# Normalising every second attention head on ScalarE in the last four batches

## The chip, the core and the metric

The kernel runs on one core of one Trainium2 chip, as one launch. A core has five engines, each with a queue of its own that it works off in order: PE (TensorE, matrix products and transposes, with the weight loads PEld beside it), DVE (VectorE), ACT (ScalarE), POOL (GpSimd) and SP (which here only issues DMAs). They wait for each other by semaphores. PE writes to PSUM, eight banks of 128 partitions x 2 KB, and DVE and ACT empty them. The metric is the device time of one execution, in microseconds; less is better.

## What is computed

Attention of 8 batches and 8 heads over 576 queries, with 16 extra "beacon" keys ahead of the 576 keys, causal over the latter; then a mixing of low rank along the sequence, and a two-layer network with ReLU over the channels, with a residual.

```python
def _attn_ref(q, k, v, beacon_k, beacon_v):          # q, k, v: 8 x 8 x 576 x 64
    k_all = np.concatenate([beacon_k, k], axis=2)    # 592 keys
    v_all = np.concatenate([beacon_v, v], axis=2)
    scores = scale * np.matmul(q, k_all.transpose(0, 1, 3, 2))
    scores = np.where(causal, -1000000000.0, scores)
    a = np.exp(scores - scores.max(-1, keepdims=True))
    a /= a.sum(-1, keepdims=True) + 1e-09
    return np.matmul(a, v_all)

def _moe_ref(x, U, V, w_ch1, w_ch2):                 # x: 8 x 576 x 512
    h = x.transpose(0, 2, 1) @ U @ V
    u = x + h.transpose(0, 2, 1)
    return u + np.maximum(u @ w_ch1, 0.0) @ w_ch2
```

## The kernel before

Heads are worked on in pairs: slot `p` is pair `p % 4` of batch `p // 4`, 32 slots in all. For a pair PE makes the transposed scores (`sps`, keys down the partitions, queries along the columns; L371 and, from the third batch on, L410 in `visit`), in four groups of blocks that lie in a bank each. ACT takes the exponential of each group into an `expt` buffer in SBUF (L419; 496, 464, 496 and 208 columns for groups 0 to 3). There are four such buffers, two slots' worth; `visit` may take groups of two neighbouring slots in one call, and group 3 of both shares a bank. DVE then takes the minimum with a mask over the diagonal blocks (L349), which sets masked entries to zero.

`av_unit` multiplies with the values. For one head it fills one bank, `po`, with five query tiles of 65 columns: 64 of the weighted sum, and one with the sum of the weights, since the values have a column of ones. DVE takes the reciprocal of the five sums (L436, 128x5, into the persistent tile `rec`), and multiplies all five tiles by it in one instruction (L437, 128x5x64, fp32 in PSUM to fp16 in `xb`, the batch's token-major attention result). With that the bank is given back.

Banks are handed out by `pst` in the order in which `emptying` gave them back, as the program is written. So each product that opens a new bank waits for the instruction that emptied that bank some steps before, on whichever engine that ran.

When a batch's four pairs are done, `turn_x` has SP transpose `xb` by DMA into `uT` (L456); DVE adds the product of low rank to it (L477). The network then runs in blocks of 512 tokens, as a queue of small units. `fill(n)` takes n of them and writes them between the parts of a slot, so that PE has work while ACT and DVE prepare the next pair. In the batches concerned a block is made with seven half-size products in place of eight, in both layers. Names that the steps below use:

- `gps` (L675): a bank of the first layer, turned into `gT` by a Relu on ACT (L683) or DVE (L681);
- `qpsA`, `qpsD`, `qpsF` (L701): banks of the first layer's seven-product form. `qpsA` grows from product to product, and after each ACT copies its state out (L720, into `kept` or `st`), which must be done before PE adds the next product to it; DVE adds that copy to `qpsD` and `qpsF` (L723), ACT ends `qpsA` with a Relu (L756);
- `mpsA` to `mpsF` (L829, L909): banks of the second layer; `mpsA` is copied out by ACT (L866, L919, L926), the others by DVE (L849).

From slot 12 on, `long_slot` sets the order by hand, by the pair's place in its batch. In the first and the second place (c = 0, 1) the `av` parts stand among `fill` calls. In the third (c = 2) the two parts are followed by `go([(p+1, 2), (p+2, 0)])`, four exponentials of 496 columns; in the fourth (c = 3) by `turn_x` and `go` with groups 2, 1 and the shared group 3, eight exponentials. The scheduler is told to keep the written order (`tc.manual_schedule`), so the order of each queue is that of the code.

Of the kernel before, what the change touches and what calls it, by code (L numbers as in the profile page):

```python
# [13 lines left out]
AF = mybir.ActivationFunctionType  # L14
ALU = mybir.AluOpType
# [3 lines left out]
P = 128  # L19
# [11 lines left out]
def kernel(  # L31
# [13 lines left out]
    nc = tc.nc  # L45
    B, H, S, D = q.shape
# [9 lines left out]
    scale = float(1.0 / (D ** 0.5))  # L56
# [6 lines left out]
    NT = NC  # L63
# [43 lines left out]
    def pst(shape, dtype, name):  # L107

        b = emptied.pop(0)
        t = psum.tile(shape, dtype, tag=f"bank{b}", name=name)  # L110
        bank_of[id(t)] = (b, t)
        return t

    def emptying(t):
        emptied.append(bank_of.pop(id(t))[0])
# [308 lines left out]
    def av_unit(b, h, ex, vs, xb):  # L424
        po = pst([P, NT, E], F32, name="po")
        for j in range(NT):
            for c in range(j + 1):
                nc.tensor.matmul(  # L428
                    po[:, j, :],
                    ex[0 : nk[c], ds(blk[(c, j)], P)],  # L430
                    vs[0 : nk[c], ds(c * H * E + h * E, E)],
                    start=(c == 0),
                    stop=(c == j),
                )
        r = rec[:, b * H + h, :, :]
        nc.vector.reciprocal(out=r, in_=po[:, :, D : D + 1])  # L436
        nc.vector.tensor_tensor(  # L437
            out=xb[:, :, ds(h * D, D)], in0=po[:, :, 0:D], in1=r.broadcast_to([P, NT, D]), op=ALU.mult
        )
        emptying(po)  # L440

    def x_into(xb, ups, cc, js, a, first):
# [798 lines left out]
    def av_of(p):  # L1241
        b, c = divmod(p, NH2)
        if c == 0:
            assert not coming or b < DT0
            xbs[b] = xbp.tile([P, NT, DM], F16, name="xb", tag="xb")
        return [
            lambda i=i: av_unit(b, 2 * c + i, expts_of(p)[i], vss[b % 2], xbs[b]) for i in range(2)
        ]
# [8 lines left out]
    DT0 = 4  # L1257
# [100 lines left out]
    with tc.manual_schedule(engines={ENG.PE, ENG.Activation, ENG.DVE, ENG.SP, ENG.Pool}):  # L1358
# [194 lines left out]
        for p in range(NP1, NP):  # L1553
            b, c = divmod(p, NH2)
# [75 lines left out]
    with tc.If(n_bad != 0, label="general"):  # L1630
        with tc.For_i(0, B, 1) as bi:
            L = qk_tiles()
            qT = qkt.tile([P, NH2, S], F16, name="qT", tag="qT")
            xb = xbp.tile([P, NT, DM], F16, name="xb", tag="xb")
# [45 lines left out]
```

## Time and profile before

| | |
|---|---|
| median of 3 runs | 331.51 us (331.44 to 334.58) |
| the profiled execution's own time | 331.11 us |
| its span in the trace | 329.4 us |
| granted TensorE clock | 1.00 throughout |

The profile is of one execution. Rows of a group give line, engine, operation, out<-in with shapes, count, busy us, mean ns of one, and the idle time before them with what ended it. Rows of the timeline give start, duration (of the merged instructions, where a count x2 or more stands behind), engine, line and shapes, and in brackets an idle time before the row and what ended it. Time counts from the start of the span. PEld is PE's weight load: it runs ahead of the products, so its waits need not hold them up. The four batches from `DT0 = 4` on have their `av` parts between 127.1 us and 258.6 us.

### The profile page before, as it was taken

The page shows a single profiled execution, that of the slowest core. Times are in us where ns is not written, and L with a number is a line of the kernel's source. Part 1 is how long each engine was busy: PE and PEld are TensorE (multiplying, and loading weights), DVE is VectorE, ACT ScalarE, POOL GpSimd, SP SyncE. Part 2 cuts the span into 40 slices and gives each one's busy share as a digit, 9 for nine tenths or more (in the row PEclk, how much of TensorE's full clock was granted, in tenths as well). Part 3 has the DMA queues.
Part 4 walks back from the last instruction along what each step waited for, and adds up shares of the span by engine and source line. Part 5 has one row for each costly group of instructions (what it writes and reads, how often), then busy time and mean ns, then how long its engine had stood idle before and what let it go on. Part 6 is the DMA issues. An engine that isn't in the chain of part 4 may idle for free.

```text
span 329.4 us, 9288 instructions
## 1 busy us (share of the span) xinstructions
PE 323.4 (98%) x3661; PEld 228.6 (69%) x3661; DVE 263.6 (80%) x610; ACT 196.8 (60%) x432; POOL 167.2 (51%) x263
## 2 busy tenths in 40 slices
PE   8899999999999999999999999999999999999996
PEld 4564555555578655876588878865777888788785
DVE  6676988668998577787778777877878998797994
ACT  5966962689972577447954796368726622722720
POOL 8985834568147960589148932960085036030030
PEclk9999999999999999999999999999999999999999
DMA  8999999999999994999999999795114321505104
GB/s 166 141 163 143 182 192 201 194 192 151 110 128 160 186 173 83 118 160 144 147 141 134 190 123 164 96 207 91 20 34 140 67 61 65 98 0 161 35 1 131
DMA packets 150558, 41.95 MB, mean 127 GB/s; under 512 B 131312, under 2 KB 149936, under 8 KB 150512
## 3 DMA queue, kind: packets, MB, share of 16 engines
q0 software_dynamic: 87568, 18.18, 75.1%
q1 hardware_dynamic: 62144, 22.41, 35.9%
q10 hardware_dynamic: 800, 0.75, 0.7%
q8 instruction: 29, 0.48, 0.6%
q14 instruction: 17, 0.14, 0.2%
HBM read 37.45 MB, written 9.44 MB: 142 GB/s over the span
## 4 chain that ended last, share of the span: by engine, by line
PE 93%; ACT 4%; DVE 1%; DMA 1%; issue 0%
PE gps L675 22%; PE po L428 9%; PE mpsA L909 9%; PE qpsA L701 6%; PE mpsD L829 6%; PE sps L410 6%; PE cps L1053 4%; PE gps L1027 4%; PE mpsE L829 3%; PE mpsC L829 3%; PE mpsB L829 3%; PE qpsD L701 3%; ACT expt L377 2%; PE mpsF L829 2%; ACT w L377 2%; PE mpsD L909 2%
## 5 line engine op out<-in xcount | busy, mean ns | idle before, releaser
L577 POOL TENSOR_TENSOR ob<-ob,ut 128x128 f32<-128x128 f32 x104 | 50.0, 511 | 120.7 <-DVE ob L849 59.4
L419 ACT ACTIVATE expt<-sps 128x496 f16<-128x496 f32 (+2 forms) x192 | 82.0, 539 | 41.8 <-PE sps L410 41.8
L675 PE MATMUL gps<-uT,w 128*128 128x512 f16 (+1 forms) x368 | 78.1, 351 | 0.0
L829 PEld LDWEIGHTS <-gT 128*128 128x128 f16 x576 | 54.3, 98 | 8.7 <-issue 2.6
L675 PEld LDWEIGHTS <-w 128*128 128x128 f16 x368 | 33.3, 98 | 25.6 <-issue 1.3
L653 DVE TENSOR_TENSOR gT<-gT 128x1024 f16<-128x1024 f16 (+3 forms) x87 | 47.0, 561 | 0.9
L239 POOL DMA_DIRECT2D vs<-in_v_dram x50 | 40.0, 817 | 14.2 <-DMA w<-in_moe_w_ch_dram 12.2
L683 ACT ACTIVATE gT<-gps 128x512 f16<-128x512 f32 x63 | 37.4, 617 | 16.0 <-PE gps L675 11.9
L428 PEld LDWEIGHTS <-expt 128*128 128x128 f16 x900 | 33.9, 98 | 8.4 <-issue 1.5
L428 PE MATMUL po<-vs,expt 128*128 128x65 f16 x900 | 36.4, 194 | 0.6 <-DVE expt L349 0.4
L909 PEld LDWEIGHTS <-gT 128*128 128x128 f16 x336 | 31.2, 98 | 3.9
L437 DVE TENSOR_TENSOR xb<-po,rec 128x320 f16<-128x320 f32 x64 | 31.4, 491 | 2.2
L349 DVE TENSOR_TENSOR expt<-expt,bigmask 128x768 f16<-128x768 f16 x56 | 31.3, 599 | 0.4 <-ACT expt L419 0.2
L720 ACT ACTIVATE kept<-qpsA 128x512 f32<-128x512 f32 x18 | 10.9, 603 | 24.0 <-PE qpsA L701 13.2
L410 PE MATMUL sps<-qT,kT 64*128 64x80 f16 (+4 forms) x288 | 22.6, 281 | 0.0
L436 DVE RECIPROCAL rec<-po 128x5 f32<-128x5 f32 x64 | 11.9, 186 | 13.0 <-PE po L428 12.8
L377 ACT ACTIVATE expt<-sps 128x496 f16<-128x496 f32 (+2 forms) x48 | 20.6, 584 | 0.7 <-PE sps L371 0.7
L909 PE MATMUL mpsA<-w,gT 128*128 128x256 f16 x160 | 19.1, 273 | 0.0
L410 PEld LDWEIGHTS <-kT 64*128 64x128 f16 x288 | 10.2, 94 | 12.8 <-issue 8.2
L681 DVE TENSOR_SCALAR gT<-gps 128x512 f16<-128x512 f32 x17 | 11.7, 689 | 8.9 <-PE gps L675 8.6
L1136 POOL DMA_DIRECT2D st<-in_q_dram x20 | 16.9, 868 | 1.0 <-DVE rec L436 0.4
L1136 POOL DMA_DIRECT2D st<-in_k_dram x20 | 16.9, 861 | 1.0 <-DVE pr L292 1.0
(165 smaller groups left out, 541.6 us busy)
## 6 DMA issues: line engine op xcount, KB each, us to landing
out_dram<-ob SPq DMA_DIRECT2D x33, 256.0 KB, 3.1
vs<-in_v_dram POOLq DMA_DIRECT2D x18, 128.0 KB, 6.9
w<-in_moe_w_ch_dram POOLq DMA_DIRECT2D x4, 512.0 KB, 6.6
w<-in_moe_w_ch_dram POOLq DMA_DIRECT2D x2, 1024.0 KB, 12.9
st<-in_k_dram POOLq DMA_DIRECT2D x12, 128.0 KB, 6.7
st<-in_q_dram POOLq DMA_DIRECT2D x12, 128.0 KB, 8.8
st<-in_k_dram POOLq DMA_DIRECT2D x4, 288.0 KB, 12.0
st<-in_q_dram POOLq DMA_DIRECT2D x4, 288.0 KB, 12.5
```

The source lines that it names most:

```text
L239: nc.gpsimd.dma_start(out=dst[a : a + nq[j], j, :, :], in_=src[hs, ds(q0[j], nq[j]), :].rearrange("h p d -> p h d"))
L377: nc.scalar.activation(out=ex[i][:, ds(AT[g], gw[g])], in_=ps[g, i][:, 0 : gw[g]], func=AF.Exp, scale=scale)
L410: nc.tensor.matmul(banks[i][:, ds(at0 + o, w)], kT(hp, c, ch), qT[hp, c, ds(qa, w)], start=True, stop=True, skip_group_check=len(unit) > 1,)
L419: nc.scalar.activation(out=at[p][3][i][:, ds(AT[g], gw[g])], in_=bank[:, ds(at0, gw[g])], func=AF.Exp, scale=scale)
L428: nc.tensor.matmul(po[:, j, :], ex[0 : nk[c], ds(blk[(c, j)], P)], vs[0 : nk[c], ds(c * H * E + h * E, E)], start=(c == 0), stop=(c == j),)
L577: nc.gpsimd.tensor_tensor(out=o[:, i, ds(c, w)], in0=x[:, i, ds(c, w)], in1=y[:, i, ds(c, w)], op=op)
L653: nc.vector.tensor_tensor(out=o[:, ds(d0, n)], in0=x[:, ds(d0, n)], in1=y[:, ds(d0, n)], op=op)
L675: nc.tensor.matmul(g[:, ds(o, w)], w1[:, cc, ts(dc, P)], uT[:, cc, ds(at, w)], start=(cc == 0 and o == 0), stop=(cc == NCC - 1), skip_grou ...
L683: nc.scalar.activation(out=cell["g"][:, dc, :], in_=g, func=AF.Relu)
L829: nc.tensor.matmul(ps, a()[:, d, ds(P * i, P)], bm[:, d, ds(c0, w)], start=fresh and d == 0 and i == 0, stop=d == HF - 1, skip_group_check ...
L909: nc.tensor.matmul(ps, a()[:, d, ds(P * i, P)], bm[:, d, ds(c0, w)], start=fresh and d == 0, stop=d == HF - 1, skip_group_check=True,)
L1136: coming.append(lambda d=dst, s=src, a=m[j] - nq[j], n=m[j], j=j: nc.gpsimd.dma_start(out=d[a:n, j, :, :], in_=s[:, ds(q0[j], nq[j]), :].r ...
```

## The change

From batch `DT0 = 4` on, the second head of each pair (`h % 2`) is multiplied by ACT. DVE still takes the reciprocal. In place of DVE's one instruction over all five query tiles there are five ACT copies of 128x64, one a tile, each with the tile's column of `rec` as a per-partition scale. The first head of each pair, the earlier batches and the fallback path stay as they are. These are 4 batches x 4 pairs = 16 heads: 16 DVE instructions go, 80 ACT instructions come.

```diff
         r = rec[:, b * H + h, :, :]
         nc.vector.reciprocal(out=r, in_=po[:, :, D : D + 1])
-        nc.vector.tensor_tensor(
-            out=xb[:, :, ds(h * D, D)], in0=po[:, :, 0:D], in1=r.broadcast_to([P, NT, D]), op=ALU.mult
-        )
+        if b >= DT0 and h % 2:
+            for j in range(NT):
+                nc.scalar.activation(
+                    out=xb[:, j, ds(h * D, D)], in_=po[:, j, 0:D], func=AF.Copy, scale=r[:, j, :]
+                )
+        else:
+            nc.vector.tensor_tensor(
+                out=xb[:, :, ds(h * D, D)], in0=po[:, :, 0:D], in1=r.broadcast_to([P, NT, D]), op=ALU.mult
+            )
         emptying(po)
```

Lines behind it have numbers higher by six in the changed file: L683, L720 and L756 are L689, L726 and L762 there.

ACT's queue at the end of slot 19 (the fourth pair of batch 4), before: the Relu that ends `qpsA`, then the eight exponentials of the next slots (numbers in the names are those of the buffers and banks), then three Relus.

```order
L756 ACTIVATE gT<-qpsA 128x2x256
L419 ACTIVATE expt_105<-sps_3128 128x496
L419 ACTIVATE expt_106<-sps_3129 128x496
L419 ACTIVATE expt_105<-sps_3136 128x464
L419 ACTIVATE expt_106<-sps_3137 128x464
L419 ACTIVATE expt_105<-sps_3140 128x208
L419 ACTIVATE expt_107<-sps_3140 128x208
L419 ACTIVATE expt_106<-sps_3141 128x208
L419 ACTIVATE expt_108<-sps_3141 128x208
L683 ACTIVATE gT<-gps 128x512 x3
```

The same place in the changed kernel:

```order
L762 ACTIVATE gT<-qpsA 128x2x256
L439 ACTIVATE xb<-po,rec 128x64 x5
L419 ACTIVATE expt_105<-sps_3144 128x496
L419 ACTIVATE expt_106<-sps_3145 128x496
L419 ACTIVATE expt_105<-sps_3152 128x464
L419 ACTIVATE expt_106<-sps_3153 128x464
L419 ACTIVATE expt_105<-sps_3156 128x208
L419 ACTIVATE expt_107<-sps_3156 128x208
L419 ACTIVATE expt_106<-sps_3157 128x208
L419 ACTIVATE expt_108<-sps_3157 128x208
L689 ACTIVATE gT<-gps 128x512 x3
```

The five copies stand ahead of the eight exponentials; nothing else has moved.

ACT's queue one slot earlier, at the end of slot 18 (the third pair), before:

```order
L720 ACTIVATE kept<-qpsA 128x512
L419 ACTIVATE expt_107<-sps_3015 128x496
L419 ACTIVATE expt_108<-sps_3016 128x496
L419 ACTIVATE expt_105<-sps_3023 128x496
L419 ACTIVATE expt_106<-sps_3024 128x496
L720 ACTIVATE kept<-qpsA 128x512
L683 ACTIVATE gT<-gps 128x512 x2
```

And in the changed kernel:

```order
L726 ACTIVATE kept<-qpsA 128x512
L439 ACTIVATE xb<-po,rec 128x64 x5
L419 ACTIVATE expt_107<-sps_3027 128x496
L419 ACTIVATE expt_108<-sps_3028 128x496
L419 ACTIVATE expt_105<-sps_3035 128x496
L419 ACTIVATE expt_106<-sps_3036 128x496
L726 ACTIVATE kept<-qpsA 128x512
L689 ACTIVATE gT<-gps 128x512 x2
```

Here they stand ahead of four exponentials and of the next copy of `qpsA`.

ACT's queue in the last two slots, 30 and 31, before:

```order
L720 ACTIVATE kept<-qpsA 128x512 x2
L683 ACTIVATE gT<-gps 128x512
L419 ACTIVATE expt_107<-sps_4912 128x496
L419 ACTIVATE expt_108<-sps_4913 128x496
L720 ACTIVATE kept<-qpsA 128x512
L683 ACTIVATE gT<-gps 128x512
L720 ACTIVATE st_115<-qpsA 128x512
L756 ACTIVATE gT<-qpsA 128x2x256
L720 ACTIVATE st_115<-qpsA 128x512
L683 ACTIVATE gT<-gps 128x512
L720 ACTIVATE st_115<-qpsA 128x512
```

And in the changed kernel:

```order
L726 ACTIVATE kept<-qpsA 128x512 x2
L439 ACTIVATE xb<-po,rec 128x64 x5
L689 ACTIVATE gT<-gps 128x512
L419 ACTIVATE expt_107<-sps_4972 128x496
L419 ACTIVATE expt_108<-sps_4973 128x496
L726 ACTIVATE kept<-qpsA 128x512
L689 ACTIVATE gT<-gps 128x512
L726 ACTIVATE st_115<-qpsA 128x512
L762 ACTIVATE gT<-qpsA 128x2x256
L726 ACTIVATE st_115<-qpsA 128x512
L689 ACTIVATE gT<-gps 128x512
L439 ACTIVATE xb<-po,rec 128x64 x5
```

The copies of slot 30 stand ahead of a Relu of `gps`, those of slot 31 ahead of the next copy of `qpsA` (the row that followed, `st_115<-qpsA`, comes behind them). DVE's queue loses one row at each of the sixteen places, PE's and SP's keep their order; where they waited for DVE's multiplication, for the bank or for `xb`, they wait for ACT.

## The prediction

> **What bounds the kernel now.** I read the page's busy times first, then the windows over the four batches that change, then who waits for whom there, then the timeline slot by slot. A slot is one head pair: 16 to 19 are batch 4, 20 to 23 batch 5, 24 to 27 batch 6, 28 to 31 batch 7. In the first row a number is busy time and a percentage its share of the span; in the second, PE's busy time stands first, DVE's third, ACT's fourth, and 1.00 is the granted clock; the third gives us in total, times, and the longest.
>
> ```profile
> PE 323.4 (98%) x3661; PEld 228.6 (69%) x3661; DVE 263.6 (80%) x610; ACT 196.8 (60%) x432; POOL 167.2 (51%) x263
> ...
> 125.00:263.00 138.00, 138.00 (x1609) 103.61 (x1609) 111.45 (x238) 86.40 (x189) 69.67 (x111) 1.00 1.12 122
> ...
> PEld L675 <- DVE xb L437: 0.9, 3, 0.5
> ...
> L437 DVE TENSOR_TENSOR xb<-po,rec 128x320 f16<-128x320 f32 x32 | 15.7, 491 | 1.1
> ```
>
> PE is busy for all 138.00 us of the stretch in which all sixteen changed heads lie. DVE's share there is 81% (111.45), ACT's 63% (86.40). PE waits for the operation that is moved, L437, three times, for 0.9 us together, and that is on its weight loads, which run ahead of the products. So faster vector work can give back 0.9 us at most, while every wait newly put in PE's way is lost for good: PE has no pause in which to catch up.
>
> **What is removed.** Half of the 32 rows of L437 go: 16 x 0.491 = 7.9 us of DVE. PE's stream hides them now, and they give nothing back. The sixteen reciprocals stay, in place.
>
> **What is added.** 80 ACT copies of 128x64. No ACT row before takes a per-partition scale, so the price is bounded by the nearest rows.
>
> ```profile
> L1189 ACT ACTIVATE kT<-tpb 128x16 f16<-128x16 f16 x1 | 0.2, 177 | 0.0
> ...
> L756 ACT ACTIVATE gT<-qpsA 128x512 f16<-128x512 f32 x6 | 3.6, 597 | 1.2 <-PE qpsA L701 1.2
> ...
> 245.10 0.34 ACT L419 ACTIVATE expt<-sps 128x208 f16<-128x208 f32 x1 [6.74 <-PE sps L410]
> ...
> 149.11 2.01 ACT L419 ACTIVATE expt<-sps 128x496 f16<-128x496 f32 x4 [1.44 <-PE sps L410]
> ...
> 155.43 2.90 ACT L419 ACTIVATE expt<-sps 128x496 f16<-128x496 f32 x8 [0.62 <-PE sps L410]
> ```
>
> Alone, 16 columns take 177 ns and 512 take 597: 0.85 ns a column, hence 177 + 48 x 0.85 = 218 ns for 64. Back to back they overlap: the second group of exponentials has 768 columns more than the first (2752 against 1984) and four instructions more, in 0.89 us more. 768 x 0.85 is 0.65; the other 0.24 is 0.06 an instruction. A 64-wide copy with full overlap then costs 0.06 + 0.054 = 0.115 us. The five copies so hold ACT for 0.58 us (full overlap) to 1.09 us (none). I take no overlap between copies, since each brings an operand of its own, whose overlap no row shows, but overlap between the last copy and the plain instruction behind it: 4 x 0.218 + 0.115 = 0.99 us. Were each as long as the next larger lone row, 0.34, it would be 4 x 0.34 + 0.115 = 1.48.
>
> The Trainium skill, "ScalarE: Activation LUTs", section "What ACT_TABLE_LOAD costs", gives 186 ns plus 0.833 ns a column with immediate operands, about 93 ns more for a pointer operand and about 93 ns of overlap back to back. By that, as an estimate, five copies hold ACT for 5 x 0.239 = 1.2 us, and the sum below would be 0.21 us dearer at each of eight places, 342.2 us in all. The trace agrees on the plain part (612 ns by the page for 512 columns, 597 in the row); no run here shows the pointer.
>
> **Where they stand.** ACT runs in order. At its place in the queue it now waits for the DVE reciprocal, then copies, and everything behind is late: exponentials, the copies of `qpsA` into `kept`, Relus, which PE needs for its banks and operands. The first copy can start about where L437 started (0.03 us after the reciprocal's end). So the delay of the next ACT instruction is L437's start + 0.99 - its present start.
>
> Third slot of a batch (18, 22, 26): four exponentials follow. First and last of the three:
>
> ```profile
> 149.12 0.18 DVE L436 RECIPROCAL rec<-po 128x5 f32<-128x5 f32 x1
> 149.33 0.49 DVE L437 TENSOR_TENSOR xb<-po,rec 128x320 f16<-128x320 f32 x1
> ...
> 150.98 0.63 ACT L720 ACTIVATE kept<-qpsA 128x512 f32<-128x512 f32 x1
> ...
> 151.82 0.60 PE L701 MATMUL qpsA<-st,lw 128*128 128x256 f16 x4
> ...
> 217.82 2.01 ACT L419 ACTIVATE expt<-sps 128x496 f16<-128x496 f32 x4 [1.48 <-PE sps L410]
> ...
> 218.00 0.49 DVE L437 TENSOR_TENSOR xb<-po,rec 128x320 f16<-128x320 f32 x1
> ```
>
> The delay is 149.33 + 0.99 - 149.11 = 1.21 and 218.00 + 0.99 - 217.82 = 1.17, 1.19 in the mean. ACT is busy without a gap to L720, so the delay reaches it whole. L720 ends at 151.61, and PE's next `qpsA` product, which adds to the bank that L720 reads, starts at 151.82: 0.21 less 0.03 for the hand-over is 0.18 of cover. PE loses 1.01 us, three times: 3.0.
>
> Fourth slot (19, 23, 27): eight exponentials follow, and the reciprocal comes after they could start.
>
> ```profile
> 156.17 0.49 DVE L437 TENSOR_TENSOR xb<-po,rec 128x320 f16<-128x320 f32 x1
> 156.69 6.95 SPq L456 DMA_TRANSPOSE uT<-xb  x5
> 156.72 2.27 PEld L675 LDWEIGHTS <-w 128*128 128x128 f16 x12 [0.47 <-DVE xb L437]
> 158.15 1.17 ACT L683 ACTIVATE gT<-gps 128x512 f16<-128x512 f32 x2
> 159.83 0.38 PE L410 MATMUL sps<-qT,kT 64*128 64x336 f16 x6
> ...
> 224.15 2.91 ACT L419 ACTIVATE expt<-sps 128x496 f16<-128x496 f32 x8 [0.62 <-PE sps L410]
> ...
> 224.66 0.49 DVE L437 TENSOR_TENSOR xb<-po,rec 128x320 f16<-128x320 f32 x1
> ...
> 226.87 1.17 ACT L683 ACTIVATE gT<-gps 128x512 f16<-128x512 f32 x2
> ...
> 228.40 0.38 PE L410 MATMUL sps<-qT,kT 64*128 64x336 f16 x6
> ```
>
> Delays: 156.17 + 0.99 - 155.43 = 1.73 and 224.66 + 0.99 - 224.15 = 1.50. The two Relus behind the exponentials end at 159.32 and 228.04 and free the banks that PE's score products take at 159.83 and 228.40; less the hand-over that is 0.48 and 0.33 of cover. PE loses 1.25 and 1.17, three times 1.21: 3.6. Within this lies the bank of `po` itself, which PE's weight load at 156.72 already awaits: it comes free at about 157.26, not 156.66. SP's transposes of `xb` start some 0.6 us later; DVE adds to what they write only some 15 us on (171.47 in the timeline):
>
> ```profile
> 171.47 1.82 DVE L477 TENSOR_TENSOR uT<-ups,uT 128x496 f16<-128x496 f32 x3
> ```
>
> Slots 30 and 31, the last two pairs, have other neighbours.
>
> ```profile
> 251.70 0.60 ACT L683 ACTIVATE gT<-gps 128x512 f16<-128x512 f32 x1 [0.73 <-PE gps L675]
> ...
> 252.40 0.49 DVE L437 TENSOR_TENSOR xb<-po,rec 128x320 f16<-128x320 f32 x1
> ...
> 253.12 0.62 ACT L720 ACTIVATE kept<-qpsA 128x512 f32<-128x512 f32 x1
> ...
> 253.77 0.69 DVE L723 TENSOR_TENSOR gT<-qpsD,kept 128x512 f16<-128x512 f32 x1 [0.88 <-ACT kept L720]
> ...
> 254.53 0.60 PE L701 MATMUL qpsD<-uT,lw 128*128 128x256 f16 x4
> ...
> 257.83 0.60 ACT L720 ACTIVATE st<-qpsA 128x512 f32<-128x512 f32 x1 [0.31 <-PE qpsA L701]
> ...
> 258.14 0.49 DVE L437 TENSOR_TENSOR xb<-po,rec 128x320 f16<-128x320 f32 x1
> ...
> 258.55 0.68 DVE L723 TENSOR_TENSOR gT<-qpsD,st 128x512 f16<-128x512 f32 x1
> ...
> 259.38 0.60 PE L701 MATMUL qpsD<-uT,st 128*128 128x256 f16 x4
> ```
>
> In 30 the delay is 252.40 + 0.99 - 251.70 = 1.69. It passes through L720 to DVE's L723, which waits for L720 now, and on to PE's `qpsD`: L723 ends at 254.46, PE starts at 254.53, 0.04 of cover. Loss 1.65. In 31 it is 258.14 + 0.99 - 257.83 = 1.30; L720 ends 0.12 before L723 starts, L723 0.15 before PE's `qpsD`, together 0.21 of cover. Loss 1.09.
>
> First and second slots (16, 20, 24, 28 and 17, 21, 25, 29) cost nothing:
>
> ```profile
> 164.73 0.49 DVE L437 TENSOR_TENSOR xb<-po,rec 128x320 f16<-128x320 f32 x1
> 165.14 0.38 ACT L919 ACTIVATE kept<-mpsA 128x256 f32<-128x256 f32 x1 [0.74 <-PE mpsA L909]
> ...
> 166.01 0.38 ACT L919 ACTIVATE kept<-mpsA 128x256 f32<-128x256 f32 x1 [0.49 <-PE mpsA L909]
> ...
> 174.01 0.49 DVE L437 TENSOR_TENSOR xb<-po,rec 128x320 f16<-128x320 f32 x1
> ...
> 176.53 0.81 ACT L419 ACTIVATE expt<-sps 128x208 f16<-128x208 f32 x3 [6.74 <-PE sps L410]
> ```
>
> In slot 20 the first L919 moves to 165.72, but the second waits for PE until 166.01 and absorbs it. In slot 21 ACT idles 6.74 us and the copies end at about 175.1, before 176.53. Were these covers gone, each block would cost up to 0.99.
>
> **Sum.** 3.0 + 3.6 + 1.65 + 1.09 = 9.4 us on the profiled execution's own 331.11: 340.5 us. That execution is 0.4 below the median of the runs, 331.51, so against that it is 2.7%.
>
> **Rivals.** (a) The copies hide: ACT's idle third takes them and PE's cover is enough. With all eight losses falling by 1 us per us of block, the total stays below 1% (3.3 us) only if the block is under 0.99 - (9.4 - 3.3)/8 = 0.23 us, 0.05 a copy, below the lower bound of 0.115. For it speaks only ACT's 63%; against it that ACT has no gap at the eight places. Time 331.5 to 334.8, not slower; chance 0.09. (b) Relief of DVE: it frees 7.9 us, but PE's waits for L437 cap the gain at 0.9: 330.2 us. More than 1% (3.3 us) would need PE waits that no row shows, against 138.00 of 138.00; I leave half of this rival's chance to it. Chance 0.04. The Trainium skill, "Perfetto Trace Analysis", section "Optimizing Scalar/DVE Operations", says that with DVE saturated some work may go to Scalar; its condition is not met at the eight places, where PE is the full engine. (c) Dearer copies, 1.48 a block: 0.49 more at eight places, 344.4 us; chance 0.13.
>
> **How the numbers follow.** The forecast has 0.74. With full overlap the block is 0.41 shorter, 3.3 us over eight places: 337.2; with none at all 0.10 longer: 341.3. The range 336.5 to 343.5 takes in both, a little more cover at the low end, and half of the way to (c). About 1% is what a measurement of this kernel can tell from no change. Faster has 0.02 (half of b), the same 0.11 (a and the rest of b), slower 0.87 (the forecast and c).
>
> **What would show it.** Right: PE idle or its loads waiting at 3 + 3 + 2 places, by about 1 us each, for ACT's copies, L720 or Relus; ACT 80 instructions more, of some 0.2 to 0.3 us; eight blocks of 0.6 to 1.1 us; nothing lost in first and second slots. Wrong: PE still without waits, blocks under 0.25 us, or PE waiting at places not named here, such as the transposes of `xb` or the masks behind the late exponentials.

## The result and the profile after

| | before | changed |
|---|---|---|
| median | 331.48 us | 341.56 us |
| lowest to highest | 331.42 to 334.58 | 340.85 to 343.16 |
| the profiled execution's own time | 331.11 us | 342.15 us |
| its span in the trace | 329.4 us | 340.5 us |

The ratio of the times is 1.0294, with a 95% interval of 1.0231 to 1.0357: slower by some 3%.

The page of the changed kernel, busy times and two of the costliest groups (columns as before; the last number is the idle time before the group, with what ended it):

```profile
PE 326.3 (96%) x3661; PEld 228.5 (67%) x3661; DVE 256.1 (75%) x594; ACT 212.7 (62%) x512; POOL 167.0 (49%) x263
...
L439 ACT ACTIVATE xb<-po,rec 128x64 f16<-128x64 f32 x80 | 18.2, 319 | 28.6 <-DVE rec L436 28.2
...
L443 DVE TENSOR_TENSOR xb<-po,rec 128x320 f16<-128x320 f32 x48 | 23.6, 492 | 1.6
```

DVE has lost 16 instructions and 7.5 us, and ACT has gained 80 instructions and 15.9 us. Neither is busy for more than 75% of the span. Nothing here looks full but PE, which does the same 3661 products as before and yet takes 11 us longer. So the question is where PE stops.

The busy time in one window of the changed kernel (PE's first, ACT's fourth), wide enough to hold all sixteen changed heads:

```profile
125.00:272.00 147.00, 140.70 (x1598) 102.75 (x1596) 102.77 (x220) 102.34 (x271) 69.73 (x111) 1.00 0.99 115
```

And whom PE waits for between 125 and 275 us (us in total, times, longest):

```profile
PE qpsA L707 <- ACT kept L726: 2.7, 4, 1.2
PE gps L681 <- ACT xb L439: 2.0, 6, 0.4
PE qpsA L707 <- ACT st L726: 0.7, 1, 0.7
PE sps L410 <- ACT gT L689: 0.6, 3, 0.2
```

Before, PE had no gap in 138 us. Now 6.3 of 147 us are gaps, and every row of the waits names ACT: its copies of `qpsA`, its Relus, and the new copies themselves, which give the bank of `po` back.

The gaps do not hold the whole loss. PE's busy time also grew, by 2.9 us, for the same products. No product is recorded as noticeably longer; but products overlap (the 368 of `gps` have a mean of 351 ns and make up only 78.3 us of busy time), and ahead of a pause the tail of the last one is not covered by a next one, and counts as busy. I therefore measured the loss as PE's lag: the start of each product in the changed trace less the start of the same product in the trace before. A step in the lag is time lost at that product. It is 1.39 us at 125 us already, ahead of the first changed head, and 10.89 at the end. Nearly all of it arose in the first 13 us. So the start-up of this execution accounts for 1.39 us of its 342.15, and the change for 9.50. (Two of the other executions took 340.85 and 340.97 us.) The steps are all at the eight foretold places:

| slots | predicted, us each | measured, us | sum predicted | sum measured |
|---|---|---|---|---|
| 18, 22, 26 | 1.01 | 1.09, 1.04, 1.11 | 3.0 | 3.2 |
| 19, 23, 27 | 1.21 | 1.10, 1.12, 1.21 | 3.6 | 3.4 |
| 30 | 1.65 | 1.70 | 1.65 | 1.7 |
| 31 | 1.09 | 1.19 | 1.09 | 1.2 |
| 16, 17, 20, 21, 24, 25, 28, 29 | 0 | 0 | 0 | 0 |

Slot 18 in the timeline of the changed kernel (start, duration, engine, line):

```profile
150.51 0.18 DVE L436 RECIPROCAL rec<-po 128x5 f32<-128x5 f32 x1
...
150.72 1.14 ACT L439 ACTIVATE xb<-po,rec 128x64 f16<-128x64 f32 x5 [1.65 <-DVE rec L436]
...
151.04 0.60 PE L707 MATMUL qpsD<-st,lw 128*128 128x256 f16 x4
...
151.72 2.03 ACT L419 ACTIVATE expt<-sps 128x496 f16<-128x496 f32 x4
...
151.91 1.89 PE L681 MATMUL gps<-uT,w 128*128 128x512 f16 x8 [0.26 <-ACT xb L439]
...
153.58 0.66 ACT L726 ACTIVATE kept<-qpsA 128x512 f32<-128x512 f32 x1
...
154.29 0.49 PE L707 MATMUL qpsA<-st,lw 128*128 128x256 f16 x3 [0.50 <-ACT kept L726]
```

The reciprocal starts 1.39 us later than before (149.12): that is the start-up, and nothing has been lost yet. ACT then waits for it, copies, and starts its exponentials 1.00 us after the first copy. The same products in the timeline of before are those at 151.82, shown in the prediction, and

```profile
149.66 0.60 PE L701 MATMUL qpsD<-st,lw 128*128 128x256 f16 x4
```

From `qpsD` to the next `qpsA` PE took 151.82 - 149.66 = 2.16 us, and now takes 154.29 - 151.04 = 3.25: 1.09 lost. The experiments use this distance again. It is lost in two pieces, first for the bank that the copies hold, then for ACT's copy of `qpsA`.

Slot 19 of the changed kernel:

```profile
158.24 0.17 DVE L436 RECIPROCAL rec<-po 128x5 f32<-128x5 f32 x1
...
158.45 1.14 ACT L439 ACTIVATE xb<-po,rec 128x64 f16<-128x64 f32 x5 [1.17 <-DVE rec L436]
...
159.64 2.75 PE L681 MATMUL gps<-uT,w 128*128 128x512 f16 x12 [0.42 <-ACT xb L439]
...
162.15 1.68 ACT L689 ACTIVATE gT<-gps 128x512 f16<-128x512 f32 x3
...
163.39 0.37 PE L410 MATMUL sps<-qT,kT 64*128 64x336 f16 x5 [0.19 <-ACT gT L689]
```

The bank again, and then, behind eight late exponentials, the Relus. Slots 30 and 31:

```profile
260.40 1.13 ACT L439 ACTIVATE xb<-po,rec 128x64 f16<-128x64 f32 x5 [1.43 <-DVE rec L436]
...
262.81 0.65 ACT L726 ACTIVATE kept<-qpsA 128x512 f32<-128x512 f32 x1
...
263.49 0.69 DVE L729 TENSOR_TENSOR gT<-qpsD,kept 128x512 f16<-128x512 f32 x1 [3.13 <-ACT kept L726]
263.51 0.60 PE L707 MATMUL qpsA<-st,w 128*128 128x256 f16 x4 [1.25 <-ACT kept L726]
...
264.24 0.60 PE L707 MATMUL qpsD<-uT,lw 128*128 128x256 f16 x4
...
267.87 1.14 ACT L439 ACTIVATE xb<-po,rec 128x64 f16<-128x64 f32 x5 [0.64 <-DVE rec L436]
...
268.87 1.11 ACT L726 ACTIVATE st<-qpsA 128x512 f32<-128x512 f32 x2
...
269.54 0.60 PE L707 MATMUL qpsA<-st,w 128*128 128x256 f16 x4 [0.74 <-ACT st L726]
```

Here too PE stops twice: first at `qpsA`, for ACT's copy of its state (1.41 us lost in slot 30, 0.90 in slot 31), then at `qpsD`, for DVE's L729, which waits for the same copy (0.29 in each).

### The profile page after: what moved, and what is told of

It is laid out like the page before. It is cut to its first block, busy times and chain, and to the rows that moved or that the text cites. A ratio compares the mean times of both kernels' runs of the same rounds, so it can differ in the third digit from the quotient of the medians.

```text
span 340.5 us, 9375 instructions
## 1 busy us (share of the span) xinstructions
PE 326.3 (96%) x3661; PEld 228.5 (67%) x3661; DVE 256.1 (75%) x594; ACT 212.7 (62%) x512; POOL 167.0 (49%) x263
## 4 chain that ended last, share of the span: by engine, by line
PE 77%; ACT 12%; DVE 6%; DMA 2%; issue 1%; ACTq 0%; DVEq 0%
PE gps L681 15%; PE mpsA L915 8%; PE po L428 7%; PE mpsD L835 6%; PE qpsA L707 5%; PE sps L410 5%; ACT expt L419 4%; PE cps L1059 4%; PE gps L1033 4%; PE mpsE L835 3%; PE mpsC L835 3%; PE mpsB L835 3%; PE qpsD L707 2%; PE mpsF L835 2%; ACT xb L439 2%; ACT expt L377 2%
## 5 line engine op out<-in xcount | busy, mean ns | idle before, releaser
L681 PE MATMUL gps<-uT,w 128*128 128x512 f16 (+1 forms) x368 | 78.3, 351 | 2.0 <-ACT xb L439 2.0
L681 PEld LDWEIGHTS <-w 128*128 128x128 f16 x368 | 33.4, 97 | 28.2 <-issue 4.6
L689 ACT ACTIVATE gT<-gps 128x512 f16<-128x512 f32 x63 | 37.2, 633 | 14.4 <-PE gps L681 13.4
L439 ACT ACTIVATE xb<-po,rec 128x64 f16<-128x64 f32 x80 | 18.2, 319 | 28.6 <-DVE rec L436 28.2
L726 ACT ACTIVATE kept<-qpsA 128x512 f32<-128x512 f32 x18 | 11.3, 627 | 24.1 <-PE qpsA L707 13.3
L443 DVE TENSOR_TENSOR xb<-po,rec 128x320 f16<-128x320 f32 x48 | 23.6, 492 | 1.6
L410 PE MATMUL sps<-qT,kT 64*128 64x80 f16 (+4 forms) x288 | 23.9, 281 | 0.6 <-ACT gT L689 0.6
```

What stands on the lines that cost most here:

```text
L410: nc.tensor.matmul(banks[i][:, ds(at0 + o, w)], kT(hp, c, ch), qT[hp, c, ds(qa, w)], start=True, stop=True, skip_group_check=len(unit) > 1,)
L681: nc.tensor.matmul(g[:, ds(o, w)], w1[:, cc, ts(dc, P)], uT[:, cc, ds(at, w)], start=(cc == 0 and o == 0), stop=(cc == NCC - 1), skip_grou ...
L689: nc.scalar.activation(out=cell["g"][:, dc, :], in_=g, func=AF.Relu)
```

## Experiments

The theory: the time is lost because ACT's queue is held, by a wait for DVE's reciprocal and by a block of five copies, at eight places where PE needs what stands behind them; relief of DVE is worth nothing. The rivals: that the whole of it is the block's length, whatever ACT waits for; that it is the wait alone; that all sixteen heads cost something; and that DVE's relief gives some of it back. Each edit is shown against the changed kernel. The times of before that ran beside them have a median of 331.34 us for four of them (first two pairs, last two, another scale, one copy) and 331.28 us for the others.

### Only the first two pairs, and only the last two

```diff
-        if b >= DT0 and h % 2:
+        if b >= DT0 and h % 2 and h < H // 2:
```

> ACT takes the second head in the first and second slot of each of the last four batches only (8 heads, 40 copies); in the third and fourth DVE multiplies as before. Theory (the loss comes at the eight places where exponentials, a Relu or a qpsA copy stand right behind the copies with no idle time of ACT): no change, 331.5 us, within 0.5 us. Rival (ACT's work as such costs PE time, in proportion to the copies): half of the loss, 336.3 us. Rival (relief of DVE is worth something): below 331 us.

Measured: 331.33 us, ratio 0.9981 (0.9941 to 1.0021). One group of the page, and the window as above:

```profile
L439 ACT ACTIVATE xb<-po,rec 128x64 f16<-128x64 f32 x40 | 9.1, 318 | 18.1 <-DVE rec L436 18.0
```

```profile
125.00:272.00 147.00, 147.00 (x1707) 111.10 (x1706) 116.32 (x243) 96.89 (x234) 72.83 (x115) 1.00 1.06 118
```

Forty copies are on ACT, it waits for DVE ahead of each block, and PE is busy for 147.00 of 147.00 us. Half of the change costs nothing. Nor does it gain: eight of DVE's multiplications, 8 x 0.492 = 3.9 us, are gone, and PE's lag is -0.19 us at 125 us, ahead of the first changed head, and -0.18 at the end.

```diff
-        if b >= DT0 and h % 2:
+        if b >= DT0 and h % 2 and h >= H // 2:
```

> The complement: ACT takes the second head in the third and fourth slot of each batch only (8 heads, 40 copies). Theory: the whole loss, 9.5 us, 341.0 us. Rival (in proportion to the copies): 336.3 us.

Measured: 340.84 us, ratio 1.0270 (1.0207 to 1.0333). The other half has all of the loss. The same instructions in the same number cost 0 or 9.5 us by where they stand.

### Another scale, to take the wait away

```diff
-                    out=xb[:, j, ds(h * D, D)], in_=po[:, j, 0:D], func=AF.Copy, scale=r[:, j, :]
+                    out=xb[:, j, ds(h * D, D)], in_=po[:, j, 0:D], func=AF.Copy, scale=rec[:, b * H + h - 1, j, :]
```

> All 80 copies as in the changed kernel, but scaled by the reciprocals of the pair's first head, which are there long before, so that ACT does not wait for this head's reciprocal; the second head's normalisation is left out with that. The block of copies keeps its 1.0 us. Theory (delay = wait for the reciprocal plus the block, less the cover): third slots nothing, fourth slots 0.2 to 0.4 us each, slot 30 0.2, slot 31 0.4, in all 1.3 us: 332.8 us. Rival (the block's length alone makes the loss): 341 us.

Measured: 340.71 us, ratio 1.0267 (1.0204 to 1.0331). The expectation missed by 8 us because the edit did not do what it was meant to do: the wait was still there. Its timeline at slot 18:

```profile
149.15 0.18 DVE L436 RECIPROCAL rec<-po 128x5 f32<-128x5 f32 x1
...
149.37 1.13 ACT L439 ACTIVATE xb<-po,rec 128x64 f16<-128x64 f32 x5 [1.65 <-DVE rec L436]
```

ACT no longer uses this reciprocal, and waits for it all the same. It reads the bank that DVE reads, and stands behind DVE in the written order. The run says nothing about the wait's worth. Two later runs bear on its reason: with no operand from `rec` at all the wait stays (the plain copies, below), and with the copies written ahead of the reciprocal it goes (the next one).

### Copies ahead of the reciprocal

```diff
-        nc.vector.reciprocal(out=r, in_=po[:, :, D : D + 1])
         if b >= DT0 and h % 2:
...
-                    out=xb[:, j, ds(h * D, D)], in_=po[:, j, 0:D], func=AF.Copy, scale=r[:, j, :]
+                    out=xb[:, j, ds(h * D, D)], in_=po[:, j, 0:D], func=AF.Copy, scale=allg
                 )
+            nc.vector.reciprocal(out=r, in_=po[:, :, D : D + 1])
         else:
+            nc.vector.reciprocal(out=r, in_=po[:, :, D : D + 1])
...
     allg = const.tile([P, 1], F32, name="allg", tag="allg")
+    nc.vector.memset(allg, 1.0 / 256)
```

> The five copies are written ahead of this head's reciprocal and scaled by a constant held in SBUF (a per-partition operand as before), so that ACT waits for PE's last product alone and DVE's reciprocal comes after ACT; the second head's normalisation is left out with that. Length of the block as in the changed kernel, 1.0 us. Theory (delay = wait for the reciprocal plus block, less cover): third slots nothing, fourth slots 0.2 to 0.35 us each, slot 30 0.1, slot 31 0.4: 1.3 us in all, 332.7 us. Rival (the block's length alone makes the loss): 341 us.

Measured: 333.65 us (332.74 to 335.23), ratio 1.0066 (1.0043 to 1.0089). Slot 18 in its timeline:

```profile
150.47 1.13 ACT L438 ACTIVATE xb<-po,allg 128x64 f16<-128x64 f32 x5 [0.25 <-PE po L428]
...
151.00 0.74 DVE L735 TENSOR_SCALAR gT<-gT 128x512 f16<-128x512 f16 x1
...
151.65 2.01 ACT L419 ACTIVATE expt<-sps 128x496 f16<-128x496 f32 x4
...
151.66 0.18 DVE L441 RECIPROCAL rec<-po 128x5 f32<-128x5 f32 x1
...
152.20 0.60 PE L708 MATMUL qpsD<-st,lw 128*128 128x256 f16 x4
...
154.37 0.60 PE L708 MATMUL qpsA<-st,lw 128*128 128x256 f16 x4
```

The five copies last as long as ever, but now wait for PE and not for DVE. They are done when DVE only gets to its reciprocal (at 151.66, 2.54 us behind the 149.12 of before, so they have not delayed it), and the exponentials start where they would have started without them (before, at 149.11; this execution had been some 2.5 us behind since 20 us). PE takes 2.17 us from `qpsD` to `qpsA`, against 2.16 before: no loss. Over the whole stretch PE lost 1.42 us: 0.33 to 0.37 in each fourth slot and 0.16 and 0.43 in the last two, less 0.2 that it won back in slots 19 and 23. So the block without the wait costs some 1.4 us, not 9.5. The timed median is 1 us higher than that explains. The profiled execution, the longest, lost its 2.5 us between 15 and 20 us: PE paused, and then the granted clock was 0.50 for 3.4 us. The fastest execution, 332.74 us, is 1.46 us above before. The others have no trace.

The same rows tell what the wait is. `po` is complete 1.2 us before DVE reaches it, because other work, L735 the last of it, stands ahead of the reciprocal in DVE's queue. And they tell where the copies went: into 1.44 us that ACT spends idle ahead of its exponentials in the kernel before (149.11 in the prediction's rows), idle time which is over when the reciprocal is done.

### The wait alone

```diff
         if b >= DT0 and h % 2:
-            for j in range(NT):
-                nc.scalar.activation(
-                    out=xb[:, j, ds(h * D, D)], in_=po[:, j, 0:D], func=AF.Copy, scale=r[:, j, :]
-                )
-        else:
-            nc.vector.tensor_tensor(
-                out=xb[:, :, ds(h * D, D)], in0=po[:, :, 0:D], in1=r.broadcast_to([P, NT, D]), op=ALU.mult
-            )
+            nc.scalar.activation(out=warm, in_=ones, func=AF.Copy, scale=r[:, 0, :])
+        nc.vector.tensor_tensor(
+            out=xb[:, :, ds(h * D, D)], in0=po[:, :, 0:D], in1=r.broadcast_to([P, NT, D]), op=ALU.mult
+        )
```

> DVE multiplies as before; where the five copies stood ACT does one activation of one column, scaled by the new reciprocal, into a scratch tile. The wait for the reciprocal stays, the block shrinks from 1.0 to about 0.15 us, and DVE frees the bank. Theory: 0.85 us less at each of eight places, from 9.5 us: 0.2 in each third slot, 0.3 in each fourth, 0.85 in slot 30, 0.3 in slot 31, 2.7 us in all: 334.1 us. Rival (the wait for DVE alone makes the loss): 341 us.

Measured: 334.37 us, ratio 1.0093 (1.0076 to 1.0110); in its trace PE lost 3.08 us over the stretch, and the execution had begun 1.13 behind. Slot 18:

```profile
150.52 0.30 ACT L438 ACTIVATE warm<-ones,rec 128x1 f16<-128x1 f16 x1 [1.71 <-DVE rec L436]
150.72 1.98 ACT L419 ACTIVATE expt<-sps 128x496 f16<-128x496 f32 x4
150.79 0.60 PE L703 MATMUL qpsD<-st,lw 128*128 128x256 f16 x4
...
153.24 0.60 PE L703 MATMUL qpsA<-st,lw 128*128 128x256 f16 x4
```

DVE multiplies as before. One column of copy into a tile that nobody reads, put behind the reciprocal, makes PE take 2.45 us here: 0.29 lost. Its block is 0.20 us. The wait (with this short block, which it cannot be had without) and the block apart cost 3.1 and 1.4 us; together they cost 9.5. Each alone is covered in part by the slack of its place; the slack can be used only once.

### The price of the block: one copy, plain copies, ten copies

```diff
-            for j in range(NT):
-                nc.scalar.activation(
-                    out=xb[:, j, ds(h * D, D)], in_=po[:, j, 0:D], func=AF.Copy, scale=r[:, j, :]
-                )
+            nc.scalar.activation(
+                out=xb[:, :, ds(h * D, D)], in_=po[:, :, 0:D], func=AF.Copy, scale=r[:, 0, :]
+            )
```

> The wait stays, the block shrinks: one ACT copy of all five tiles (128x320) with the first tile's reciprocal as scale, in place of five; the other four tiles' own scaling is left out. By the copy's measured 0.31 us at 64 columns and 0.83 ns a column it should take 0.53 us alone and hold up the next one by 0.41, against 1.00. Theory: 0.59 us less at each of eight places, 4.7 of 9.5 us: 336.3 us. Rival (handing the bank and the xb to ACT behind the reciprocal costs, however short the copies): 341 us.

Measured: 335.85 us, ratio 1.0118 (1.0056 to 1.0180). One instruction over the same 320 columns, all scaled by the first tile's reciprocal, so that this is a price and not a replacement:

```profile
L438 ACT ACTIVATE xb<-po,rec 128x320 f16<-128x320 f32 x16 | 8.4, 527 | 28.5 <-DVE rec L436 28.4
```

Slot 18 in its timeline:

```profile
149.31 0.53 ACT L438 ACTIVATE xb<-po,rec 128x320 f16<-128x320 f32 x1 [1.65 <-DVE rec L436]
149.74 2.00 ACT L419 ACTIVATE expt<-sps 128x496 f16<-128x496 f32 x4
```

It holds ACT for 0.43 us, and half of the loss is gone: PE lost 4.6 us in the stretch, 0.47 of them at this slot.

```diff
-                    out=xb[:, j, ds(h * D, D)], in_=po[:, j, 0:D], func=AF.Copy, scale=r[:, j, :]
+                    out=xb[:, j, ds(h * D, D)], in_=po[:, j, 0:D], func=AF.Copy, scale=1.0 / 256
```

> Five copies behind the reciprocal as in the changed kernel, but with an immediate scale; the second head's normalisation is left out with that. It takes the per-partition operand away and leaves count, width and wait. Theory: back to back such a copy costs 0.10 to 0.12 us as the rows of the kernel before gave it, not 0.20; block 0.52 to 0.6 us, 0.4 to 0.48 less at eight places: 337.1 to 337.8 us. Rival (the operand costs nothing; five short copies cost 0.2 each whatever the scale): 341 us.

Measured: 338.10 us, ratio 1.0222 (1.0199 to 1.0246). Its copies between 125 and 275 us, and its timeline at slot 18:

```profile
L439 ACT ACTIVATE xb<-po 128x64 f16<-128x64 f32 x80 | 11.0, 234 | 29.4 <-DVE rec L436 29.0 <-DMA uT<-xb 0.3
```

```profile
149.23 0.69 ACT L439 ACTIVATE xb<-po 128x64 f16<-128x64 f32 x5 [1.65 <-DVE rec L436]
...
149.56 0.60 PE L707 MATMUL qpsD<-st,lw 128*128 128x256 f16 x4
...
149.76 2.06 ACT L419 ACTIVATE expt<-sps 128x496 f16<-128x496 f32 x4
...
152.36 0.60 PE L707 MATMUL qpsA<-st,lw 128*128 128x256 f16 x4 [0.48 <-ACT kept L726]
```

The copies have the same columns and the same wait, but no operand per partition. They are 85 ns shorter (234 against 319), and follow each other more closely: the fifth copy starts 0.43 us behind the first (at 149.66), 0.108 us a copy, where in the changed kernel it starts 0.80 us behind (at 151.53), 0.201 a copy. The block is 0.53 us, and PE takes 2.80 here: 0.64 lost. The time is 0.3 us above the upper end of what was expected; in two of the three fourth slots, 19 and 23, PE lost 1.1 us, as much as in the changed kernel. There DVE's reciprocal came 0.23 and 0.28 us later than PE's lag explains: the DVE instruction ahead of it (L734, on `gT`) took 0.90 and 0.89 us, where it had taken 0.67 and 0.61 before. In slot 27, where it took 0.43 in all three kernels, PE lost 0.78. Less these 0.5 us the time lies inside the range expected. Why that instruction's length varies is not shown.

```diff
-                nc.scalar.activation(
-                    out=xb[:, j, ds(h * D, D)], in_=po[:, j, 0:D], func=AF.Copy, scale=r[:, j, :]
-                )
+                for x in range(0, D, D // 2):
+                    nc.scalar.activation(
+                        out=xb[:, j, ds(h * D + x, D // 2)], in_=po[:, j, ds(x, D // 2)], func=AF.Copy, scale=r[:, j, :]
+                    )
```

> Each copy is cut in two of 32 columns: ten copies a head, everything else as in the changed kernel. 32 columns less is 0.03 us less a copy: ten at 0.17 make a block of 1.7 us in place of 1.0. Theory: 0.7 us more at eight places: 346.6 us, and more if the first and second slots lose their cover. Rival (the loss comes once a head, by handing over between engines): 341 us.

Measured: 347.72 us, ratio 1.0501 (1.0482 to 1.0521). Slot 18:

```profile
149.86 1.89 ACT L440 ACTIVATE xb<-po,rec 128x32 f16<-128x32 f32 x10 [1.65 <-DVE rec L436]
...
150.19 0.60 PE L708 MATMUL qpsD<-st,lw 128*128 128x256 f16 x4
...
151.57 2.07 ACT L419 ACTIVATE expt<-sps 128x496 f16<-128x496 f32 x4
...
154.18 0.60 PE L708 MATMUL qpsA<-st,lw 128*128 128x256 f16 x4 [0.49 <-ACT kept L727]
```

Here the block is 1.71 us and PE takes 3.99: 1.83 lost. The time is 1.1 us above what was expected, and 1.0 of this lies in places that had cost nothing: in the first slots 20, 24 and 28 PE's score products now come 0.32 to 0.34 us late, behind the last copy that frees their bank. Their cover was real, and it ends somewhere between a block of 1.0 and one of 1.7 us.

Put side by side, slot 18 gives a rule for this place:

| | wait alone | one copy | plain copies | changed kernel | ten copies |
|---|---|---|---|---|---|
| block, us | 0.20 | 0.43 | 0.53 | 1.00 | 1.71 |
| lost at `qpsA`, us | 0.29 | 0.47 | 0.64 | 1.09 | 1.83 |

The loss is the block plus 0.04 to 0.12 us, over blocks of one, five and ten instructions. By the prediction's numbers it is the block plus 0.22 (how late the first copy starts) less 0.18 (cover), which is 0.04 more than the block. No one of these versions beats the kernel before. Whether a reciprocal placed earlier in DVE's queue would take the wait out of a version that normalises was not tried; by the copies ahead of the reciprocal it would leave no gain over before, since PE has no gap to close.

## Why the prediction was right

**The bound.** "PE has no pause in which to catch up" holds: in the changed kernel no step of the lag is won back (0.13 us returns behind each fourth slot, and is lost again before the next step). In the runs with one copy, with the copies first and with the wait alone it won back 0.14 us in slot 19 and 0.07 in slot 23, at products whose weight loads had waited for L437 before. The first two pairs alone show the other side of it, 147.00 of 147.00 us busy, with ACT doing forty copies beside.

**The places.** The eight places and the eight free ones came out as named, by the two half changes and by the lag. The sum is 9.5 against 9.4 us. The third slots lost 0.2 us more in all than foretold, the fourth 0.2 less: in slots 19 and 23 DVE's L734, ahead of the reciprocal, took 0.47 and 0.46 us in place of 0.67 and 0.61, so the copies could start that much sooner than the prediction had it. The prediction saw only one way at the third slots, through the copy of `qpsA`. PE in fact stops twice, first for the bank that the copies hold (0.43 us at slot 18), then for the copy (0.66). That their sum agrees is, given the block, no accident: both are parts of one delay of ACT's queue, and the last wait sets the total. In the fourth slots the split is likewise bank, then Relus (0.45, then 0.17 and 0.48 at slot 19). In slots 30 and 31 the prediction's way, through DVE to `qpsD`, is the one that ended last; that PE would first stop at `qpsA`, for ACT's copy itself, it did not see.

**The block.** Its size was right, 0.99 us predicted and 1.00 measured. The way to it was wrong at the step "I take no overlap between copies, since each brings an operand of its own". The copies do overlap, by about 0.319 - 0.201 = 0.118 us, and the plain ones by nearly the same, 0.234 - 0.108 = 0.126. What was missing on the other side is the operand's price, 85 ns in a copy's length. A copy is 0.319 us and not 0.218, but the next one starts 0.201 us behind it. The two errors cancel, so it is luck that the block, and with it the total, came out this close. The plain copies show what it would have been without the operand: 0.53 us, a little under the prediction's full overlap of 0.58.

The Trainium skill, "ScalarE: Activation LUTs", section "What ACT_TABLE_LOAD costs", has this price at about 93 ns for a pointer operand, and the runs agree (85 ns in length, 93 from start to start). The estimate from the Trainium skill, 0.239 us from copy to copy, 1.2 us a block and 342.2 us, was dearer than the measured 0.201 and 1.00 us by both of its terms: an overlap of about 93 ns, where the runs show 118, and a length of 332 ns, an estimate from its figures, where they show 319.

**The removed work.** That 7.9 us of DVE "give nothing back" is shown for half of it by the first two pairs: 3.9 us less of DVE, and a ratio of 0.9981 with 1 well inside its interval. In the last two pairs no relief shows either: the 0.14 and 0.07 us that PE won back there in slots 19 and 23 came with the wait alone too, where DVE multiplies as before.

**The rivals.** That the copies hide (a) falls with the measured block, 1.00 us against the 0.23 at which that rival would decide. Relief of DVE (b) falls with the first two pairs. Dearer copies (c) fall with the block. The wait is something that the prediction had in its sum, as the lateness of the first copy, without saying how much hung on it: without it the same copies cost 1.4 us.

**Two slips in the working.** "ACT has no gap at the eight places" is not what its rows show: ACT idles 1.44 us right ahead of the exponentials of slot 18, 0.62 in slot 19, 0.73 and 0.31 in slots 30 and 31. The copies cannot use that time because the reciprocal is done only when that time is over; put ahead of the reciprocal, they did, and in the third slots cost nothing. And the range's upper end, 343.5 us, lies some three quarters of the way from 340.5 to (c) at 344.4, not half of it; at a measured 341.56 nothing hangs on this.

## What to carry to other kernels

An engine that is idle for a third of the time takes work for nothing only in its idle places, and only work that is ready while they last: the same forty copies cost 0 in one half of the slots and 9.5 us in the other, and all eighty cost 1.4 us where they did not wait for DVE. Where the bounding engine never pauses, price a move at each place as the wait plus the block that the new work puts into the taker's queue, less the slack of what stands behind it, and count that slack once. Hand over in few wide instructions (0.43 us of queue for one copy, 1.00 for five, 1.71 for ten, over the same columns), and look at what stands ahead of the producer of its operand in the other queue.

## What the runs showed that was not expected

- An operand per partition made each ACT copy of 128x64 85 ns longer (319 against 234 ns) and set the copies 93 ns further apart (0.201 against 0.108 us from start to start).
- ACT's copies waited for DVE's reciprocal of the same bank without using its result: 29.0 us of waits with plain copies that take nothing from DVE, where the changed kernel's, which need it, had 28.2. Written ahead of the reciprocal, they waited for PE instead. This is an order of the program. No run lets the two engines read the bank at once, so whether it could be dropped is not shown.
- The same DVE instruction on `gT` took 0.43 to 0.90 us in the fourth slots, by the kernel and the slot, and moved the reciprocal behind it. Why is not shown.
- Of 9.5 us lost by PE, the gaps in its busy time show 6.3; its busy time itself rose from 323.4 to 326.3 us for the same 3661 products. Matched starts gave the whole.
